# Linear attention and SwiGLU, four layers: attention regrouped through xnᵀφ(k), and a list scheduler for every engine but TensorE

## The chip, the cores and the metric

The kernel runs on one core of one Trainium2 chip. The metric is the device time of one execution in microseconds (us). Five engines work side by side, each through its own instruction queue in order: TensorE (PE; its weight loads are shown as PEld), VectorE (DVE), ScalarE (ACT), GpSimd (POOL) and SyncE (SP), the last of which only issues transfers here. They wait for one another through semaphores.

## What is computed

The input x has 2048 tokens of width 512, in bf16. Two blocks, attention A and feed-forward B, are applied in turn, twice:

```python
x = x + A(layernorm(x));  x = x + B(layernorm(x))
x = x + A(layernorm(x));  x = x + B(layernorm(x))

def A(x):                                 # 32 heads of width 16
    q, k, v = split(x @ wqkv)             # wqkv: 512 x 1536
    phi = lambda t: where(t > 0, t + 1, exp(t)) + 1e-6
    kv = einsum("bhsd,bhse->bhde", phi(k), v)
    z  = einsum("bhsd->bhd", phi(k))
    o  = einsum("bhqd,bhde->bhqe", phi(q), kv) / (phi(q) . z + 1e-6)
    return o @ wo                         # wo: 512 x 512

def B(x):
    return (silu(x @ w_gate) * (x @ w_up)) @ w_down   # 512 x 1792, 1792 x 512
```

The attention is linear: no token-by-token matrix is formed. Per head a 16 x 16 matrix `kv` and a vector `z` are summed over all tokens, and only then can any token's output be formed.

## The kernel before

Tokens are cut into 16 tiles of 128 (`T`), four of which form a group of 512 (`TG` = 4, `G` = 4 groups). Width 512 is cut into `NC` = 4 chunks of 128, the inner width 1792 into `NF` = 14. All weights and X stay in SBUF.

*Norm, for every layer and tile.* DVE takes the statistics (`fe_stats`, L350 and L351). GpSimd forms the reciprocal deviation and the shift for four tiles at once (`fe_rstd`, L361 to L368; for the first four tiles one by one). ACT writes the normalised tile `xn` (`fe_apply`, L378, a ring of four buffers), and a DMA transpose on SP's queue writes it to `xnT` (`fe_T`), the layout that TensorE needs.

*Attention, first pass.* Per tile `p1_proj` (L409) makes k and v, eight matmuls of 512 columns, in banks 0 to 3. phi is ACT's exponential (L388), DVE's min and add (L392), and DVE's max and add (L395). ACT copies v to SBUF (L425). Per group `p1_kvacc_pe` (L443) multiplies phi(k) by v with a column of ones, 16 matmuls of 129 columns, threaded between the projections; DVE adds the four groups' results up. `kv_final` masks the product to the heads' blocks (`KVbd`, `Z8`).

*Attention, second pass.* Per group and chunk `p2_q` (L484) makes q, transposed, in banks 0 and 1; phi follows. `p2_den_pe` (L508, 16 matmuls of 8 columns) makes the denominators, DVE takes the reciprocal (L514, L517), TensorE transposes it (L522), ACT copies it (L528), TensorE spreads it over the heads' rows (L535), and DVE multiplies q by it (L544). `p2_o_pe` (L550) multiplies by `KVbd`, ACT copies the result (L555), and `wo_pe` (L563) multiplies by `Wo`; a fifth matmul with the identity (L566) adds X, and ACT writes X back (L571).

*Feed-forward.* Per group and inner chunk `gu_pe` (L583) makes gate and up, eight matmuls, in one of three pairs of banks. ACT takes tanh(g/2) (L594); DVE forms (tanh + 1) g (L601) and 0.5 times that times up (L604), which is `hT`. After 14 chunks `dn_pe` (L613) makes each tile's 14 down matmuls, and DVE adds X (L620; L624 in the last layer, whose result goes to DRAM).

*What sets the order.* `Tasks.run` walks all tasks in rounds; a task is emitted when all that it depends on were emitted in an earlier round, and each kind has a quota per round. Every engine's queue is then in the order of emission; `Sched` turns reads and writes of named buffers into semaphore waits. TensorE is the engine the rounds are built around: projections, q blocks and gate blocks each wait for their predecessor and for a free ring slot. Weights come in on GpSimd's queue, chunk after chunk behind the first layer's transposes; chunks of one weight share a name, so the next waits for the one before.

## Time and profile before

| | us |
|---|---|
| Times of three runs | 489.0, 490.49, 491.71 |
| Median | 490.49 |
| Profiled execution, span from first to last instruction | 491.9 |
| PE busy | 445.4 |
| DVE busy | 318.2 |
| ACT busy | 207.0 |
| POOL busy | 43.5 |

The profiled execution is another execution than the three timed ones; it has no time of its own beside its span. The span is 1.4 us above the median run. TensorE's matmuls overlap: one of 512 columns is shown with 379 ns, but in a row of them one starts every 216 ns, so a busy TensorE need not be at its peak; elapsed time has to be compared with counts.

### The profile page before, as it was taken

Reading aid. Unit: us, or ns where it says so; the run is one execution under the profiler, and the core shown is the slowest. Engines: PE = TensorE matmul, PEld = TensorE weight load, DVE = VectorE, ACT = ScalarE, POOL = GpSimd, SP = SyncE. Lnnn points to the kernel's source line nnn. Section 1 sums busy time; section 2 is a strip of 40 time slices with the busy share of each in tenths; the row PEclk is TensorE's granted clock in tenths of the full one; section 3 lists DMA queues with packets and bytes.
Section 4 is the critical chain, followed back from the end, with each engine's and each line's share of the span. In section 5 each row is a group of like instructions: output and inputs, shape, how many; then the busy total and the mean of one; then the engine's idle time right before and its main releaser. Section 6 shows DMA issues by size and latency. Waiting matters only on the chain.

```text
span 491.9 us, 6354 instructions
## 1 busy us (share of the span) xinstructions
PE 445.4 (91%) x2196; PEld 203.3 (41%) x2240; DVE 318.2 (65%) x586; ACT 207.0 (42%) x345; POOL 43.5 (9%) x113
## 2 busy tenths in 40 slices
PE   0898758989999999999999975889999999999997
PEld 0343323434344444444444542444434444444443
DVE  4843768728956846846846566872995574573672
ACT  2685434685541511511508643577553131131120
POOL 6431110101200100100101000010120000000000
...
GB/s 296 134 152 157 160 65 0 1 44 17 69 44 0 45 1 1 43 1 0 44 1 45 0 0 1 1 0 45 26 59 65 22 2 23 21 0 23 21 2 43
DMA packets 41135, 20.60 MB, mean 42 GB/s; under 512 B 35408, under 2 KB 39504, under 8 KB 41104
## 3 DMA queue, kind: packets, MB, share of 16 engines
...
q10 hardware_dynamic: 528, 1.57, 0.9%
...
q14 instruction: 13, 0.11, 0.1%
...
## 4 chain that ended last, share of the span: by engine, by line
PE 75%; DVE 12%; DMA 4%; ACT 3%; issue 3%; POOL 2%; POOLq 0%; ACTq 0%; DVEq 0%
PE pb L583 33%; PE pb L613 19%; PE pb L409 10%; DMA sb<-sb 4%; PE pb L563 4%; PE pb L484 3%; DVE sb L395 3%; DVE sb L350 2%; DVE sb L604 2%; DVE sb L601 2%; PE pb L443 1%; DVE sb L544 1%; DVE sb L517 1%; ACT sb L378 1%; PE pb L566 1%
## 5 line engine op out<-in xcount | busy, mean ns | idle before, releaser
L583 PE MATMUL pb<-sb 128*128 128x512 bf16 x879 | 198.0, 379 | 2.3 <-DVE sb L601 1.4
L594 ACT ACTIVATE sb<-pb 128x512 bf16<-128x512 f32 x112 | 66.7, 596 | 168.2 <-PE pb L583 157.9
L583 PEld LDWEIGHTS pb<-sb 128*128 128x128 bf16 x896 | 87.1, 98 | 109.0 <-ACT sb L594 4.2
L613 PE MATMUL pb<-sb 128*128 128x512 bf16 x438 | 100.2, 379 | 0.5
L601 DVE SCALAR_TENSOR_TENSOR sb<-sb,pb 128x512 bf16<-128x512 bf16 x112 | 76.1, 680 | 25.5 <-ACT sb L594 25.5
L409 PE MATMUL pb<-sb 128*128 128x512 bf16 x250 | 65.6, 401 | 17.9 <-DMA sb<-sb 17.2
L604 DVE SCALAR_TENSOR_TENSOR sb<-sb,pb 128x512 bf16<-128x512 bf16 x112 | 76.9, 687 | 3.8
L613 PEld LDWEIGHTS pb<-sb 128*128 128x128 bf16 x448 | 43.8, 98 | 52.8
L388 ACT ACTIVATE sb<-pb 128x512 bf16<-128x512 f32 x64 | 38.2, 596 | 61.2 <-PE pb L484 29.9
L378 ACT ACTIVATE sb<-sb 128x512 bf16<-128x512 bf16 x64 | 51.7, 808 | 14.4 <-POOL sb L368 13.9
L484 PE MATMUL pb<-sb 128*128 128x512 bf16 x123 | 32.8, 387 | 18.5 <-DVE sb L395 17.4
L350 DVE BATCH_NORM_STATS2 sb<-sb 128x6 f32<-128x512 bf16 x64 | 43.4, 678 | 6.9 <-DMA sb<-in_A_x_dram 6.8
L409 PEld LDWEIGHTS pb<-sb 128*128 128x128 bf16 x256 | 25.5, 102 | 52.0 <-issue 21.4
L395 DVE SCALAR_TENSOR_TENSOR sb<-pb,sb 128x512 bf16<-128x512 f32 x64 | 44.3, 692 | 2.2
L624 DVE TENSOR_TENSOR sb<-pb,sb 128x512 bf16<-128x512 f32 x16 | 11.1, 692 | 43.0 <-PE pb L613 43.0
L620 DVE TENSOR_TENSOR sb<-pb,sb 128x512 bf16<-128x512 f32 x16 | 11.1, 692 | 36.4 <-PE pb L613 36.4
L392 DVE TENSOR_SCALAR sb<-sb 128x512 bf16<-128x512 bf16 x64 | 18.1, 282 | 24.6 <-ACT sb L388 24.6
L544 DVE TENSOR_TENSOR sb<-pb,sb 128x512 bf16<-128x512 f32 x32 | 21.9, 684 | 16.2 <-PE pb L535 15.9
L563 PE MATMUL pb<-sb 128*128 128x512 bf16 x124 | 32.1, 379 | 0.1
L361 POOL TENSOR_SCALAR sb<-sb 128x4 f32<-128x4 f32 (+1 forms) x19 | 4.3, 226 | 278.0 <-DVE sb L351 277.7
L484 PEld LDWEIGHTS pb<-sb 128*128 128x128 bf16 x128 | 10.8, 98 | 35.0 <-ACT sb L388 10.8
L443 PE MATMUL pb<-sb 128*128 128x129 bf16 x128 | 23.6, 220 | 1.2 <-DVE sb L395 1.0
...
## 6 DMA issues: line engine op xcount, KB each, us to landing
...
sb<-sb SPq DMA_TRANSPOSE x64, 2.5
...
```

What stands on the lines that cost most here:

```text
L350: op("dve", lambda v: v.bn_stats(stats[:, t, :], Xin[:, t, :]), reads=[f"X{t}"], writes=[f"stats{t}"])
L378: op("act", lambda a: a.activation(out=xn[b][:], in_=Xin[:, t, :], func=ACT.Identity, bias=nmr[:, t:t + 1], scale=rstd[:, t:t + 1]), reads ...
L388: op("act", lambda a: a.activation(out=etmp[e][:], in_=PB[pb][:], func=ACT.Exp), reads=[f"pb{pb}"], writes=[f"etmp{e}"])
L395: op("dve", lambda v: v.scalar_tensor_tensor(out=dst_ap, in0=PB[pb][:], scalar=0.0, in1=etmp[e][:], op0=ALU.max, op1=ALU.add), reads=[f"pb ...
L409: op("pe", lambda pe, pb=pb, col0=col0, c=c: pe.matmul(PB[pb][:], lhsT=xnT[:, c, t * P:(t + 1) * P], rhs=Wqkv[:, c, col0:col0 + 512], star ...
L484: op("pe", lambda pe, c=c: pe.matmul(PB[pb][:], lhsT=Wqkv[:, c, j * P:(j + 1) * P], rhs=xnT[:, c, g * 512:(g + 1) * 512], start=(c == 0), ...
L563: op("pe", lambda pe, c=c: pe.matmul(PB[pb][:], lhsT=oT[ob][:, c, tl * P:(tl + 1) * P], rhs=Wo[:, c, :], start=(c == 0), stop=False), read ...
L583: op("pe", lambda pe, pb=pb, W=W, c=c: pe.matmul(PB[pb][:], lhsT=W[:, c, j * P:(j + 1) * P], rhs=xnT[:, c, g * 512:(g + 1) * 512], start=( ...
L594: op("act", lambda a: a.activation(out=tht[s][:], in_=PB[pbg][:], func=ACT.Tanh, scale=0.5), reads=[f"pb{pbg}"], writes=[f"sg{s}"])
L601: op("dve", lambda v: v.scalar_tensor_tensor(out=gst[s][:], in0=tht[s][:], scalar=1.0, in1=PB[pbg][:], op0=ALU.add, op1=ALU.mult), reads=[ ...
L604: op("dve", lambda v: v.scalar_tensor_tensor(out=hT[hb][:, j, :], in0=gst[s][:], scalar=0.5, in1=PB[pbu][:], op0=ALU.mult, op1=ALU.mult), ...
L613: op("pe", lambda pe, j=j: pe.matmul(PB[pb][:], lhsT=hT[hb][:, j, tl * P:(tl + 1) * P], rhs=Wd[:, j, :], start=(j == 0), stop=(j == NF - 1 ...
```

## The change

Attention is regrouped. Since v = xn Wv, phi(k)ᵀ v is (xnᵀ phi(k))ᵀ Wv; so v is not formed per token. `g_acc` sums G = xnᵀ phi(k) over all 16 tiles in four banks. `kvt` forms Wvᵀ G per chunk and masks it to the heads' blocks, and `m_mm` multiplies that by `Wo`, so that M = KV Wo. z is summed by matmuls with a column of ones (`z_acc`). phi(q) is divided by its denominator before M: the reciprocal is repeated over a head's 16 columns by ACT, transposed by a DMA on SP's queue, and multiplied into phi(q) by DVE (`den`). `wo` then needs four matmuls per tile, and DVE adds X.

The norm's GpSimd part runs per tile. Tiles 0 to 3 of the first layer are normalised by DVE and transposed by TensorE; all others go by DMA transposes as before. Normalised attention tiles are all kept (`xnA`), since `g_acc` reads them; `xnT` becomes six buffers of a group each. Gate and up use four banks (two pairs), k and q two, everything else two. `hT` holds twice the value, the halving is in the residual, and tanh is kept in fp32.

TensorE's order is written out by hand: 14 matmuls on zeros at the start; the last q block and eight `wo` tiles of each attention, and twelve k projections of the third layer, are threaded through the gate blocks. The order on the other engines comes from a list scheduler over modelled durations: at each step the instruction that can start first goes next, ties by a deadline computed back from TensorE's order.

```diff
+    def schedule(self):
...
+        while left:
+            best = None
+            for e in self.ENGINES:
+                if e == "pe":
+                    if pe_at < len(pe_q) and nd[pe_q[pe_at].i] == 0:
+                        o = pe_q[pe_at]
+                        s = max(free[e], rt_of[o.i])
+                        if best is None or s < best[0]:
+                            best = (s, o)
+                    continue
+                cand = None
+                for o in avail[e]:
+                    s = max(free[e], rt_of[o.i])
+                    key = (s, o.dead, o.i)
+                    if cand is None or key < cand[0]:
+                        cand = (key, o)
...
+        r_gu = Ring([0, 1, 2, 3])
+        r_kq = Ring([4, 5])
+        r_tok = Ring([6, 7])
...
+        def ln(L, t, apply="act", pe_t=False):
...
+            if apply == "act":
+                op("pool", lambda p: p.tensor_scalar(out=nmr[:, t:t + 1], in0=mv[:, t, 0:1],
+                                                     scalar1=rstd[:, t:t + 1], scalar2=-1.0,
...
+                op("act", lambda a: a.activation(out=b_ap, in_=X[:, t, :], func=ACT.Identity,
...
+            if pe_t:
+                pb = r_kq.take()
+                tp = PB[pb][:].bitcast(BF16)
+                for c in range(NC):
+                    op("pe", lambda e, c=c: e.transpose(out=tp[:, c * P:(c + 1) * P],
...
+                op("dve", lambda v: v.tensor_copy(out=dst, in_=tp[:, 0:512].rearrange("p (c k) -> p c k", c=NC)),
...
+            else:
+                op("sp", lambda e: e.dma_start(dst, b_ap, transpose=True), r=[bk], w=[f"xt{sl}_{tl}"],
+                   occ=0.1, lat=2.5, dma="t")
...
+        def k_proj(L, t):
...
+                mm(pb, xnT[sl][:, c, tl * P:(tl + 1) * P], Wqkv[:, c, D:2 * D], c == 0, c == NC - 1,
+                   r=[f"xt{sl}_{tl}", "Wk"], w=[f"pb{pb}"])
+            phi(pb, pk[t][:], f"pk{t}", "stt")
+
+        def g_acc(t):
+            for c in range(NC):
+                mm(c, xnA[:, t, c * P:(c + 1) * P], pk[t][:], t == 0, t == T - 1,
+                   r=[f"xa{t}", f"pk{t}"], w=[f"pb{c}"])
...
+        def z_acc(L, tiles):
...
+                    mm(pb, pk[t][:, c * P:(c + 1) * P], ones[:], t == 0 and c == 0, t == T - 1,
...
+        def g_copy():
             for c in range(NC):
+                evac(c, GT[:, c, :], f"GT{c}", "act" if c % 2 == 0 else "dve")
+
+        def kvt():
...
+                    mm(pb, Wqkv[:, k, 2 * D + c * P:2 * D + (c + 1) * P], GT[:, k, c * P:(c + 1) * P],
...
+        def m_mm():
+            for c in range(NC):
+                mm(c, KVT[:, c, :], Wo[:, c, :], True, True, r=["KVT", "Wo"], w=[f"pb{c}"])
+                evac(c, Mo[:, c, :], f"Mo{c}", "act" if c % 2 == 0 else "dve")
...
+        def den(L, g):
...
+            op("dve", lambda v: v.reciprocal(out=rtok[d][:], in_=dsb[d][:]), r=[f"dsb{d}"], w=[f"rtok{d}"],
...
+            for tl in range(TG):
+                q = r_rrep.take()
+                op("act", lambda a, tl=tl, q=q: a.activation(
...
+                op("sp", lambda e, tl=tl, q=q: e.dma_start(RT[R][:, :, tl * P:(tl + 1) * P], rrep[q][:],
+                                                           transpose=True),
...
+            for j in range(NC):
+                b = pq_of[L, g, j]
+                op("dve", lambda v, j=j, b=b: v.tensor_tensor(out=pq[b][:], in0=pq[b][:], in1=RT[R][:, j, :],
...
+        def wo(L, t):
...
+                mm(pb, pq[n][:, tl * P:(tl + 1) * P], Mo[:, c, :], c == 0, c == NC - 1,
...
+        warm = r_tok.take()
+        for i in range(14):
+            mm(warm, zero[:, 0:P], zero, True, True, r=[f"h1_{NF - 1}"], w=[f"pb{warm}"], occ=0.427)
+        for t in range(2):
+            ln(0, t, apply="dve", pe_t=True)
+        late_consts([pr.ops[-1]])
+        for t in range(2, TG):
+            ln(0, t, apply="dve", pe_t=True)
+        for t in range(TG, T):
+            ln(0, t)
+        for w_ in weights[0:2]:
+            w_([])
...
+        for t in range(T):
+            k_proj(0, t)
+            load_next(1)
+            if t >= LAG:
+                g_acc(t - LAG)
+
+        for L in (0, 2):
+            if L == 0:
+                q_proj(L, 0, 0)
+                g_acc(T - 2)
+                q_proj(L, 0, 1)
+                g_acc(T - 1)
+                g_copy()
+                z_acc(L, range(0, T))
+                z_fin(L)
+            q_proj(L, 0, 2)
+            q_proj(L, 0, 3)
+            kvt()
+            q_proj(L, 1, 0)
+            q_proj(L, 1, 1)
+            m_mm()
+            den(L, 0)
+            q_proj(L, 1, 2)
+            q_proj(L, 1, 3)
+            den(L, 1)
+            q_proj(L, 2, 0)
+            q_proj(L, 2, 1)
+            q_proj(L, 2, 2)
+            q_proj(L, 2, 3)
+            for t in range(0, TG):
+                wo(L, t)
+            den(L, 2)
+            for t in range(TG, 2 * TG):
+                wo(L, t)
+            for g in range(G):
+                main = [B(gu, L + 1, g, j) for j in range(NF)] + [B(dn, L + 1, t) for t in range(TG * g, TG * (g + 1))]
+                fill = []
                 if g == 0:
+                    fill += [B(wo, L, t) for t in range(2 * TG, 3 * TG)]
+                    fill += [B(q_proj, L, 3, j) for j in range(NC)] + [B(den, L, 3)]
+                if g == 1:
+                    fill += [B(wo, L, t) for t in range(3 * TG, 4 * TG)]
+                if L == 0 and g >= 1:
+                    fill += [B(k_proj, L + 2, t) for t in range(TG * (g - 1), TG * g)]
+                run(weave(main, fill, 2, NF))
             if L == 0:
+                for t in range(2 * TG, 3 * TG):
+                    g_acc(t - 2 * TG)
+                for t in range(TG, 3 * TG):
+                    g_acc(t)
+                q_proj(2, 0, 0)
+                for t in range(3 * TG, T):
+                    k_proj(2, t)
+                    if t > 3 * TG:
+                        g_acc(t - 1)
+                z_acc(2, range(0, T - 1))
+                q_proj(2, 0, 1)
+                g_acc(T - 1)
+                g_copy()
...
```

Each `wo` tile is followed by the norm of that tile for the feed-forward, and each down tile by the norm for the next attention. The first load is `Wk` (the middle third of `Wqkv`), on ACT's queue; q's and v's thirds come at once on GpSimd's queue, and each later weight chunk waits for the phi of one tile of the first k projection.

1147 lines of the change are left out of this document (465 added, 682 removed).

## The prediction

> **What bounds the kernel now.** I read the totals first, then the stretches, then the chain and the waits in the stretches where TensorE is idle.
>
> The page's totals:
> ```profile
> PE 445.4 (91%) x2196; PEld 203.3 (41%) x2240; DVE 318.2 (65%) x586; ACT 207.0 (42%) x345; POOL 43.5 (9%) x113
> ```
> Busy time by stretch; I cut at the first projection, the last one, the first `Wo` matmul, and the first gate matmul of each layer:
> ```profile
> core 0: us, PE busy (x) PEld busy (x) DVE busy (x) ACT busy (x) POOL busy (x), PEclk, DMA share, GB/s
> 0.00:14.00 14.00, 0.03 (x1) 0.06 (x2) 6.85 (x17) 4.41 (x5) 9.67 (x42) 1.00 0.91 283
> 14.00:53.30 39.30, 35.38 (x173) 16.07 (x177) 21.89 (x51) 26.16 (x44) 11.17 (x21) 0.96 0.69 144
> 53.30:85.70 32.40, 22.37 (x147) 10.19 (x149) 24.76 (x53) 13.06 (x23) 2.22 (x3) 0.95 0.21 69
> 85.70:110.30 24.60, 23.16 (x123) 10.72 (x124) 13.18 (x26) 18.42 (x33) 1.71 (x4) 1.00 0.11 22
> 110.30:256.70 146.40, 144.94 (x659) 65.48 (x672) 102.24 (x175) 50.82 (x81) 10.20 (x24) 1.00 0.12 22
> 256.70:287.30 30.60, 30.43 (x175) 15.09 (x177) 18.58 (x40) 20.59 (x35) 1.70 (x4) 1.00 0.09 18
> 287.30:317.70 30.40, 20.88 (x147) 9.59 (x149) 24.50 (x53) 12.92 (x23) 0.00 (x0) 1.00 0.01 1
> 317.70:342.30 24.60, 23.03 (x122) 10.69 (x124) 13.14 (x26) 18.42 (x33) 1.70 (x4) 1.00 0.13 23
> 342.30:488.90 146.60, 145.19 (x660) 65.37 (x671) 92.34 (x147) 42.23 (x69) 5.11 (x12) 1.00 0.10 25
> 488.90:491.90 3.00, 0.00 (x0) 0.00 (x0) 0.69 (x1) 0.00 (x0) 0.00 (x0) 0.85 0.13 44
> ```
> Prices of TensorE's work, from the chain of waits (first two rows) and the timeline:
> ```profile
> 144.20 3.02 PE pb L613 x14
> 29.60 0.06 PE pb L443
> ...
> 64.00 0.55 PE L508 MATMUL pb<-sb 128*128 128x8 bf16 x16
> 64.41 1.02 PE L484 MATMUL pb<-sb 128*128 128x512 bf16 x4
> ...
> 67.75 0.60 PE L522 MATMUL pb<-sb 128*32 128x128 f32 x4
> 68.18 1.03 PE L484 MATMUL pb<-sb 128*128 128x512 bf16 x4
> ```
> A 512-column matmul takes 3.02/14 = 0.2157 us, one of 129 columns 0.06, one of 8 columns 0.41/16 = 0.026, a small transpose 0.43/4 = 0.108. The loops issue 1952 + 128 + 128 + 32 of these: 421.0 + 7.7 + 3.3 + 3.5 = 435.5 us of work in a span of 491.9. So 56.4 us are lost. By stretch, elapsed minus work: 14.0 before the first matmul; 8.8 in the first k/v pass; 12.0 and 10.0 in the two q stretches; 2.6 twice in the `Wo` stretches; 1.5 and 1.6 in the MLPs; 0.1 in the second k/v pass; 3.0 at the end. TensorE's own work is the bound of the MLPs; the losses lie in the attention layers.
>
> Chain of waits at the start, and one row of the waits:
> ```profile
> 7.33 0.82 ACT sb L378
> 8.17 5.66 DMA sb<-sb
> 13.97 4.93 PE pb L409 x12
> 18.91 5.83 DMA sb<-sb
> ...
> 36.29 7.44 DMA sb<-sb
> 43.86 5.50 PE pb L409 x17
> ```
> ```profile
> PE pb L484 <- DVE sb L395: 17.4, 15, 2.3
> ```
> The first pass loses time to DMA transposes that land late beside the loads, and to a half clock: the first 12 matmuls took 4.93/12 = 0.41 us each. The q stretches wait for DVE's phi: 15 waits, 1.16 us each.
>
> **The change, part by part.** *TensorE's work.* Per attention layer the v projection and `KV` (64 + 64 short) become `g_acc` (64), `z_acc` (64 of one column), `kvt` (16 of 128) and `m_mm` (4); the reciprocal's transposes, its spreading (16), `o` (16) and X through the identity (16) go. q, the k projection, `den` and 64 `Wo` matmuls stay. Wide ones fall from 304 to 260, so 1864 in all, with the MLPs' 1344 unchanged: 402.1 us. `kvt` costs 32 x 0.06 = 1.9 and `den` 3.3. No row has a one-column matmul; it lies between nothing and the 0.06 row, nearest to the 8-column row: 128 x 0.026 = 3.3. Total 410.6, that is 24.9 us less (bounds 20.5 to 28.2).
>
> *Start.* Tiles 0 to 3 are transposed on TensorE and the first load is `Wk`, a third of `Wqkv`. But TensorE's queue is in order, and the first projection stands behind all four tiles.
> ```profile
> 5.79 0.24 POOL L361 TENSOR_SCALAR sb<-sb 128x1 f32<-128x1 f32 x1
> 6.12 0.58 POOL L364 TENSOR_TENSOR sb<-sb 128x1 f32<-128x1 f32 x1
> ...
> 7.76 0.69 DVE L350 BATCH_NORM_STATS2 sb<-sb 128x6 f32<-128x512 bf16 x1 [3.80 <-DMA sb<-in_A_x_dram]
> ...
> 8.58 0.66 DVE L350 BATCH_NORM_STATS2 sb<-sb 128x6 f32<-128x512 bf16 x1
> ...
> 9.38 0.66 DVE L350 BATCH_NORM_STATS2 sb<-sb 128x6 f32<-128x512 bf16 x1
> ```
> Four tiles and `Wk` are 1.0 MB, about 3.5 us at the 283 GB/s of the first stretch; with a share for the other queues tile 3 is there at about 6.7. Statistics (0.8), GpSimd (two steps, 5.79 to 6.70, about 0.9), normalising, transposing and copying add 2.8: first projection at 9.5 (bounds 8 and 13, the latter if tile 3 comes as late as now). Fourteen zero matmuls at about 0.41 us run from 1.5 to some 6 us and pay the slow clock early, which saves 12 x (0.41 - 0.216) = 2.3 if the clock holds across the gap. The 17 matmuls at 43.86 follow a gap of 2.3 us and took 0.32 each, so it may not. The Trainium skill, "TensorE: Matmul & The Clock Gate", Part 1 and Part 4, says the clock halves after an idle window of about 3.4 us and that transposes do not count as activity; by that the 2.3 us would be paid again at 9.5.
>
> *First pass.* Projections and `g_acc` alternate, 1.73 us per tile. Twelve tiles still go by DMA transposes beside 13 weight loads, each now released by a tile's phi and up to four in flight on the GpSimd queue, where the LN arithmetic of later tiles stands behind them. Loss between 1 (transposes run ahead, no ring of four `xn` buffers holds them) and the present 9: I take 4.
>
> *The stretch from g to the first gate matmul.* The MLP gets q block 3 and eight `wo` tiles as filling; here stay 12 q projections, `kvt`, `m_mm`, three `den` and eight `wo`. DVE rows:
> ```profile
> L395 DVE SCALAR_TENSOR_TENSOR sb<-pb,sb 128x512 bf16<-128x512 f32 x64 | 44.3, 692 | 2.2
> L544 DVE TENSOR_TENSOR sb<-pb,sb 128x512 bf16<-128x512 f32 x32 | 21.9, 684 | 16.2 <-PE pb L535 15.9
> L392 DVE TENSOR_SCALAR sb<-sb 128x512 bf16<-128x512 bf16 x64 | 18.1, 282 | 24.6 <-ACT sb L388 24.6
> L517 DVE RECIPROCAL sb<-sb 128x128 f32<-128x128 f32 x8 | 7.6, 954 | 0.3
> ```
> Back to back they overlap a little (timeline, DVE):
> ```profile
> 164.25 0.68 DVE L601 SCALAR_TENSOR_TENSOR sb<-sb,pb 128x512 bf16<-128x512 bf16 x1
> 164.97 0.69 DVE L604 SCALAR_TENSOR_TENSOR sb<-sb,pb 128x512 bf16<-128x512 bf16 x1
> 165.57 0.68 DVE L601 SCALAR_TENSOR_TENSOR sb<-sb,pb 128x512 bf16<-128x512 bf16 x1
> ```
> so an independent one occupies 0.60 to 0.61, a gate/up pair 1.32, and a tile's statistics 0.80 (8.58 to 9.38). A phi is 0.28 + 0.61 = 0.89. The new product of q with the reciprocal has both inputs in SBUF as bf16: no row; between 0.28 (L392) and 0.68 (L544, from PSUM); I take 0.35, nearest to L392. "VectorE: DVE Perf Modes" of the Trainium skill, in its perf-mode tier table, gives such a product two results per cycle, an estimated 0.33 us; the sum would not move by 1 us.
>
> DVE: 12 phi 10.7, evictions of G and M and the mask 3.0, `z_fin` 0.2, three `den` with four products each 3 x (0.28 + 0.95 + 1.4) = 7.9, eight residuals with statistics 8 x 1.41 = 11.3; sum 33.1. TensorE in the same stretch: 12 q and 2 g 12.1, z 1.7, `kvt` and M 1.9, `den` 1.2, `wo` 6.9; 23.8. DVE is the bound: loss 9.3, taken as 10 (3 if statistics slip into the MLP, 15 if DVE fills 85% only; the q stretches now fill 76 and 81%). In layer 2 the two first q, two g and z lie earlier: 31.1 against 18.7, loss 12. The residual moves from ACT to DVE, v's copies and `o`'s go; ACT has room.
>
> *Reciprocals.* `den`, reciprocal, four ACT copies, four DMA transposes, four products. Of transposes:
> ```profile
> L99 SPq DMA_TRANSPOSE sb<-sb x64: 1188/1191/2302, 8.2 to 375.7; - x64
> sb<-sb SPq DMA_TRANSPOSE x64, 2.5
> ```
> SP's queue takes 1.19 us for each, in order with LN's. The chain is 0.28 + 0.95 + 0.6 + 4 x 1.19 + 1.3 + 1.4 = 9.3 us; from `den(0)` to `wo(0)` DVE has 9.2 us to do (two reciprocals with their additions 2.5, six phi 5.3, the products 1.4). It is hidden, barely, and only because DVE is the bound.
>
> *MLPs.* Four instead of six banks for gate and up. With filling, group 0 has on DVE 14 x 1.32 + 4 x 1.41 + 4 x 0.89 + 2.6 = 30.3 us against 24.2 + 6.9 + 0.4 = 31.5 on TensorE, and statistics left over from `wo` may spill in; group 1 of layer 1 is as tight. I take 5 and 4 us (bounds 1.5, as now, and 20). *Layer 1 to 2:* 12 `g_acc` (10.4 us) cover the last tiles' norm and transposes (residual 0.7, statistics 0.8, GpSimd 1, ACT 0.8 as in the L378 row, DMA 2.5); 2 lost. *End:* unchanged, 3.0.
>
> Sum: 410.6 + 9.5 + 4 + 10 + 5 + 2 + 12 + 4 + 3 = 460.1 as a span. The profiled span of 491.9 is 1.4 us above the median run, 490.49; so 458.7, say 459.
>
> **The rivals.** *A, DVE's surplus is absorbed.* Statistics and products are done in the down projections, where DVE has 12.1 us with 4 x 1.41 of work. For it: the MLP stretch shows DVE busy 102 of 146 us. Against it: `wo` needs the products at once. Losses 9 + 2 + 4 + 2 + 1 + 5 + 2 + 3 = 28: span 438.6, time 437.
>
> *B, the smaller ring holds the MLP.* This row gives ACT's part:
> ```profile
> L594 ACT ACTIVATE sb<-pb 128x512 bf16<-128x512 f32 x112 | 66.7, 596 | 168.2 <-PE pb L583 157.9 <-DVE sb L350 5.7 <-DVE sb L601 4.7
> ```
> An up bank is free 0.86 + 0.16 + 0.60 + 0.71 + 0.69 + 0.1 = 3.1 us after its block began; two blocks on, it is wanted at 4.3 (with three pairs at 6.0). A residual with statistics (1.4) in between exceeds the slack of 1.2 by 0.2: over 112 blocks 22 us, of which 6 are counted: 475. For it: PE's waits on DVE exist already with three pairs. Against it: half the blocks have no filling. "Perfetto Trace Analysis" of the Trainium skill (Identifying Performance Opportunities) reads a repeating gap on the saturated engine as too few buffers; no run here shows it in the MLP.
>
> *C, slower: head of line on DVE.* DVE's order is fixed from modelled times. An instruction that stands at its head with a late operand holds every gate product behind it. Place: the MLPs' groups with filling. Price: 1.16 us, the mean wait of the L484 row. It decides from 33/1.16 = 28 such events beyond those counted, one in four gate blocks; at 40 the time is 505. Against it: TensorE's order is fixed too, and lateness moves all queues alike.
>
> *D, no change:* the same at about 28 events; 490. That the change does not remove the work it says is excluded by the counted loops.
>
> **How the numbers follow.** Forecast 0.42 (its own range 448 to 470), A 0.27, B 0.18, C 0.09, D 0.04. The range 434 to 484 leaves out a little of A and B, and C and D. No change means within 0.5% (488 to 493), about what can be told apart here: faster 0.87, same 0.04, slower 0.09.
>
> **What would show it.** Right: about 1864 wide matmuls; first projection near 9.5 us; in the stretch from the last projection to the first gate matmul DVE over 85% busy and PE waiting for DVE; MLPs near 171 and 160 us. Wrong: PE waits on DMA transposes in front of `wo`, or a gap in nearly every gate block (B), or DVE waiting for ACT or DMA while PE waits for DVE (C), or those stretches near 25 us (A).

## The result, and the profile after

The changed kernel takes 475.98 us (median of 4 runs, 473.24 to 478.77); the kernel before, run beside it, 491.1 (489.0 to 492.85). The ratio is 0.9687, 95% interval 0.9621 to 0.9752: 3.1% faster. The forecast was 459 us, a gain of 31.5; measured are 15.1. The sign is right and the size is missed by half.

Totals of the page, and busy time by stretch, of the changed kernel. The cuts are the first projection, the first q block, the first gate of layer 1, the first `g_acc` of layer 2, the third q block of layer 2, the first gate of layer 3 and the last matmul; the columns are those of the table of before.
```profile
PE 435.2 (91%) x2182; PEld 194.2 (41%) x2182; DVE 327.8 (69%) x613; ACT 171.6 (36%) x277; POOL 77.2 (16%) x214
```
```profile
0.00:15.30 15.30, 6.68 (x31) 3.17 (x32) 7.37 (x21) 0.86 (x1) 6.87 (x23) 0.86 0.75 240
15.30:48.44 33.14, 28.62 (x123) 11.37 (x122) 20.96 (x51) 18.42 (x29) 18.04 (x46) 0.96 0.82 168
48.44:89.35 40.91, 30.42 (x222) 13.43 (x221) 32.01 (x70) 18.29 (x33) 7.36 (x19) 0.83 0.34 90
89.35:257.50 168.15, 167.96 (x784) 75.89 (x785) 127.44 (x223) 64.97 (x102) 26.88 (x77) 0.99 0.14 27
257.50:279.66 22.16, 21.09 (x154) 9.91 (x153) 6.73 (x14) 5.32 (x9) 1.32 (x4) 1.00 0.09 17
279.66:315.95 36.29, 24.25 (x146) 9.90 (x144) 29.28 (x66) 17.31 (x31) 5.84 (x18) 0.86 0.22 44
315.95:473.60 157.65, 156.22 (x736) 70.56 (x736) 103.36 (x169) 46.40 (x76) 10.93 (x31) 1.00 0.13 30
473.60:477.00 3.40, 0.00 (x0) 0.00 (x0) 0.69 (x1) 0.00 (x0) 0.00 (x0) 1.00 0.11 39
```
Elapsed minus TensorE's work (0.2157 us for each wide matmul, the forecast's prices for the others) is the loss of a stretch:

| stretch | elapsed | work | loss | forecast |
|---|---|---|---|---|
| start | 15.3 | 0 | 15.3 | 9.5 |
| first pass | 33.1 | 25.9 | 7.2 | 4 |
| layer 0, q to first gate | 40.9 | 23.8 | 17.1 | 10 |
| MLP of layer 1 | 168.2 | 166.1 | 2.0 | 5 |
| layer 1 to 2 | 22.2 | 20.6 | 1.6 | 2 |
| layer 2, q to first gate | 36.3 | 18.7 | 17.6 | 12 |
| MLP of layer 3 | 157.7 | 155.7 | 1.9 | 4 |
| end | 3.4 | 0 | 3.4 | 3 |

The whole miss lies in four rows: 5.8 + 3.2 + 7.1 + 5.6 = 21.7 us, less 5.5 that the two MLPs and the stretch from layer 1 to 2 do better. In the q stretches TensorE's granted clock is 0.83 and 0.86, where the kernel before had 0.95 and 1.00, and DVE is busy 78 and 81% of the time.

What TensorE waits for in layer 0's stretch (waits view; total, times, longest), and what DVE waits for there:
```profile
PE pb L343 <- DVE pq L459: 4.4, 6, 2.6
PE pb L343 <- DMA xnT<-xnB: 2.3, 1, 2.3
PE pb L343 <- DVE pq L562: 2.3, 1, 2.3
PE pb L343 <- ACT etmp L454: 0.8, 1, 0.8
PE pb L343 <- DVE X L573: 0.8, 1, 0.8
```
```profile
DVE etmp L456 <- ACT etmp L454: 7.4, 8, 1.8
```
Ten waits make 10.6 of the 17.1 us. Most of the rest is half clock behind the long ones: in three rows, 8, 4 and 16 wide matmuls take 3.57, 1.86 and 6.26 us, together some 5.6 us more than at 0.2157 each. DVE itself is kept waiting by ACT's exponentials. The timeline shows the longest wait as a chain through four queues (start, duration, in brackets the idle time before and its releaser):
```profile
62.55 2.19 ACT L553 ACTIVATE rrep<-rtok 128x512 bf16<-128x512 f32 x4 [0.83 <-DVE rtok L548]
...
64.64 0.57 ACT L454 ACTIVATE etmp<-pb 128x512 bf16<-128x512 f32 x1
65.25 0.29 DVE L456 TENSOR_SCALAR etmp<-etmp 128x512 bf16<-128x512 bf16 x1 [1.79 <-ACT etmp L454]
65.64 0.69 DVE L459 SCALAR_TENSOR_TENSOR pq<-pb,etmp 128x512 bf16<-128x512 f32 x1
66.39 0.27 PE L343 MATMUL pb<-Zm,pq 128*128 128x8 bf16 x4 [2.62 <-DVE pq L459]
66.52 3.57 PE L343 MATMUL pb<-xnT,Wqkv 128*128 128x512 bf16 x8
...
70.29 1.86 PE L343 MATMUL pb<-xnT,Wqkv 128*128 128x512 bf16 x4 [0.20 <-DVE pq L459]
```
ACT's four copies of the reciprocals stand in front of the exponential of q(1,3). DVE waits 1.79 us for that exponential, TensorE 2.62 us for DVE, and the next eight wide matmuls take 3.57 us in place of 1.73, at half clock. Another chain of this kind ends at the first gate:
```profile
78.79 1.28 DVE L408 BATCH_NORM_STATS2 stats<-X 128x6 f32<-128x512 bf16 x2
...
80.03 7.96 SPq L445 DMA_TRANSPOSE xnT<-xnB  x4
80.24 0.87 POOL L410 TENSOR_SCALAR vpe<-mv 128x1 f32<-128x1 f32 x3 [1.19 <-DVE mv L409]
80.28 1.09 DVE L562 TENSOR_TENSOR pq<-pq,RT 128x512 bf16<-128x512 bf16 x3
80.76 6.26 PE L343 MATMUL pb<-Mo,pq 128*128 128x512 bf16 x16 [2.26 <-DVE pq L562]
81.07 1.76 POOL L413 TENSOR_TENSOR rstd<-vpe,negh 128x1 f32<-128x1 f32 x3
...
82.93 0.74 POOL L422 TENSOR_SCALAR nmr<-mv,rstd 128x1 f32<-128x1 f32 x3
83.29 2.22 ACT L426 ACTIVATE xnB<-X,nmr,rstd 128x512 bf16<-128x512 bf16 x3 [3.33 <-POOL nmr L422]
...
89.35 1.71 PE L343 MATMUL pb<-xnT,Wg 128*128 128x512 bf16 x4 [2.33 <-DMA xnT<-xnB]
```
The products of group 1 start at 80.28, behind the residuals and statistics of earlier tiles, so `wo(4)` waits 2.26 us and its 16 matmuls run at half clock (6.26 us for 3.45 of work). The norm of tiles 1 to 3 needs 3.4 us on GpSimd, step by step for three tiles, then ACT, then SP, and the gate comes 11 us after `wo(3)`.

### The profile page after: what moved, and what is told of

Same layout as the page of the kernel before. It is cut to its first block, busy times and chain, and to the rows that moved or that the text cites. A ratio compares the mean times of both kernels' runs of the same rounds, so it can differ in the third digit from the quotient of the medians.

```text
span 477.0 us, 6447 instructions
## 1 busy us (share of the span) xinstructions
PE 435.2 (91%) x2182; PEld 194.2 (41%) x2182; DVE 327.8 (69%) x613; ACT 171.6 (36%) x277; POOL 77.2 (16%) x214
## 4 chain that ended last, share of the span: by engine, by line
PE 73%; DVE 9%; DMA 7%; SPq 5%; POOL 2%; issue 2%; ACT 2%; DVEq 0%; ACTq 0%; POOLq 0%
PE pb L343 72%; DMA xnT<-xnA 3%; SPq L557 3%; DMA RT<-rrep 2%; SPq L445 2%; DVE stats L408 2%; DVE pq L459 2%; DVE X L573 1%; DMA X<-in_A_x_dram 1%; POOL rstd L413 1%; DVE pq L562 1%; ACT etmp L454 1%; DVE etmp L456 1%; POOL vpe L410 1%; DVE Mo L500 1%
## 5 line engine op out<-in xcount | busy, mean ns | idle before, releaser
L343 PE MATMUL pb<-xnT,Wg 128*128 128x512 bf16 x448 | 115.8, 381 | 5.5 <-DMA xnT<-xnB 5.3
L343 PE MATMUL pb<-xnT,Wu 128*128 128x512 bf16 x448 | 115.9, 381 | 1.4 <-DVE hT L596 1.4
L591 ACT ACTIVATE tht<-pb 128x512 f32<-128x512 f32 x112 | 66.5, 595 | 124.5 <-PE pb L343 112.9
L343 PE MATMUL pb<-Wd,hT 128*128 128x512 bf16 x448 | 98.0, 379 | 0.0
L593 DVE SCALAR_TENSOR_TENSOR tht<-tht,pb 128x512 f32<-128x512 f32 x112 | 76.5, 683 | 26.3 <-ACT tht L591 25.7
L596 DVE TENSOR_TENSOR hT<-tht,pb 128x512 bf16<-128x512 f32 x112 | 76.8, 686 | 9.8 <-DVE mv L409 0.4
L343 PEld LDWEIGHTS pb<-xnT,Wg 128*128 128x128 bf16 x448 | 43.8, 98 | 59.6 <-issue 7.4
L343 PEld LDWEIGHTS pb<-xnT,Wu 128*128 128x128 bf16 x448 | 44.0, 98 | 55.2 <-DVE hT L596 2.1
L343 PEld LDWEIGHTS pb<-Wd,hT 128*128 128x128 bf16 x448 | 43.7, 98 | 52.4
L454 ACT ACTIVATE etmp<-pb 128x512 bf16<-128x512 f32 x64 | 37.9, 594 | 64.4 <-PE pb L343 57.5
L408 DVE BATCH_NORM_STATS2 stats<-X 128x6 f32<-128x512 bf16 x64 | 42.8, 682 | 7.4 <-DMA X<-in_A_x_dram 6.6
L343 PE MATMUL pb<-Mo,pq 128*128 128x512 bf16 x128 | 36.1, 419 | 6.0 <-DVE pq L562 4.5
L426 ACT ACTIVATE xnB<-X,nmr,rstd 128x512 bf16<-128x512 bf16 x32 | 25.3, 809 | 36.8 <-POOL nmr L422 30.6
L343 PE MATMUL pb<-pk,xnA 128*128 128x512 bf16 x128 | 31.1, 379 | 0.0
## 6 DMA issues: line engine op xcount, KB each, us to landing
Wu<-in_B_w_up_dram POOLq DMA_DIRECT2D x4, 448.0 KB, 10.7
```

The lines of the kernel that those rows point to most:

```text
L343: return op("pe", lambda e: e.matmul(o_ap, lhsT=lhsT, rhs=rhs, start=start, stop=stop, skip_group_check=skip), r=r, w=w, occ=occ, lat=occ ...
L408: op("dve", lambda v: v.bn_stats(stats[:, t, :], X[:, t, :]), r=[xk], w=[f"st{t}"], occ=0.6)
L426: op("act", lambda a: a.activation(out=b_ap, in_=X[:, t, :], func=ACT.Identity, bias=nmr[:, t:t + 1], scale=rstd[:, t:t + 1]), r=[xk, f"nm ...
L454: op("act", lambda a: a.activation(out=etmp[e][:], in_=PB[pb][:], func=ACT.Exp), r=[f"pb{pb}"], w=[f"e{e}"], occ=0.485, lat=0.6)
L591: op("act", lambda e: e.activation(out=tht[a][:], in_=PB[pg][:], func=ACT.Tanh, scale=0.5), r=[f"pb{pg}"], w=[f"th{a}"], occ=0.485, lat=0.6)
L593: op("dve", lambda v: v.scalar_tensor_tensor(out=tht[a][:], in0=tht[a][:], scalar=1.0, in1=PB[pg][:], op0=ALU.add, op1=ALU.mult), r=[f"pb{ ...
```

## The experiments

Two theories stood at first: L, that the reciprocals' chain and the half clock behind its waits make the surplus loss, and D, that DVE's load does, as the forecast had it. Each kernel was timed beside the kernel before, in 4 runs (6 for e1). Where stretches are compared they are differences of the starts of the same matmuls in one profiled execution each:

| kernel | median us | ratio, 95% interval | start | first pass | layer 0: q to gate | layer 2: second q block to gate |
|---|---|---|---|---|---|---|
| changed kernel | 475.98 | 0.9687 (0.9621-0.9752) | 15.3 | 33.2 | 40.9 | 38.1 |
| a1 | 475.94 | 0.9671 (0.9629-0.9713) | 14.7 | 31.2 | 40.9 | 38.1 |
| a2 | 471.92 | 0.9589 (0.9556-0.9622) | 15.3 | 35.4 | 38.0 | 34.2 |
| a3 | 483.87 | 0.9839 (0.9813-0.9865) | 15.2 | 35.6 | 42.4 | 40.1 |
| a4 | 474.59 | 0.9662 (0.9618-0.9705) | 15.2 | 31.0 | 42.6 | 37.8 |
| b1 | 475.95 | 0.9666 (0.9624-0.9707) | 15.3 | 30.9 | 40.6* | 37.6* |
| b2 | 470.08 | 0.9559 (0.9496-0.9622) | 15.2 | 33.6 | 35.2* | 33.6* |
| b3 | 480.29 | 0.9770 (0.9697-0.9843) | 12.4 | 38.6 | 41.0 | 37.9 |
| b4 | 473.51 | 0.9629 (0.9589-0.9669) | 15.2 | 29.2 | 43.1 | 37.6 |
| c1 | 470.24 | 0.9577 (0.9531-0.9622) | 15.0 | 33.0 | 41.1* | 30.6* |
| c2 | 468.30 | 0.9527 (0.9478-0.9576) | 15.1 | 29.4 | 40.6* | 30.6* |
| c3 | 466.06 | 0.9479 (0.9437-0.9522) | 12.5 | 29.1 | 39.4* | 30.6* |
| c4 | 471.48 | 0.9591 (0.9550-0.9632) | 15.3 | 29.2 | 40.3* | 33.1* |
| d1 | 500.66 | 1.0214 (1.0151-1.0277) | 18.3 | 44.8 | 44.5 | 42.0 |
| d2 | 477.26 | 0.9725 (0.9650-0.9800) | 15.3 | 30.9 | 40.7 | 37.5 |
| d3 | 474.44 | 0.9649 (0.9594-0.9704) | 14.7 | 37.2 | 38.7* | 32.1* |
| d4 | 476.40 | 0.9684 (0.9622-0.9745) | 13.1 | 34.8 | 41.9* | 34.0* |
| e1 | 459.75 | 0.9353 (0.9312-0.9394) | 12.4 | 29.2 | 36.1* | 30.7* |
| e2 | 463.19 | 0.9434 (0.9390-0.9479) | 12.4 | 29.6 | 40.1* | 30.1* |

\* less the work that was moved into the stretch from the MLP (3.45 us; in d4 another 3.86).

The first pass is not steady: where nothing bearing on it was changed (changed kernel, a2, a3, b1, b2) it took 30.9 to 35.6 us. That is why the stretches are looked at and not the medians alone.

### First round: one suspect each

**a1**, the first loads in program order:
```diff
-                    key = (s, o.dead, o.i)
+                    key = (s, o.i if o.dma == "d" else o.dead, o.i)
```


> The list scheduler's choice among ready loads goes by the order in which they are written instead of by deadline; so tile 0 is loaded first instead of fourth (in the changed kernel the deadlines put tiles 3, 2, 1, 0 in this order on SP's queue, and DVE's first statistics, those of tile 0, wait until 7.8 us). If the order of the loads holds the start: the statistics of tiles 0 to 2 are done by the time the fourth load lands at about 7.8, and the first projection comes at about 11.8 instead of 15.3 us; the time falls by 3 to 4 us (ratio to the changed kernel about 0.993). If the last of the four loads or the bandwidth holds it, whatever the order: first projection at 15, time unchanged within 1 us.

The order of the loads alone is worth 0.6 us of start. Tile 0's statistics came at 3.07 us (7.82 in the changed kernel), but DVE's timeline shows what took their place:
```profile
8.55 0.38 DVE L430 TENSOR_SCALAR xnA<-X,mv,rstd 128x512 bf16<-128x512 bf16 x1
10.68 0.69 DVE L408 BATCH_NORM_STATS2 stats<-X 128x6 f32<-128x512 bf16 x1 [1.75 <-DMA X<-in_A_x_dram]
11.29 0.40 DVE L430 TENSOR_SCALAR xnA<-X,mv,rstd 128x512 bf16<-128x512 bf16 x1
```
The statistics of tile 4, whose load lands at 10.7, stand at the head of DVE's queue in front of tile 1's normalisation.

**a2**, no division: the copies, their transposes and the four products of `den` are left out, so q is not divided.
```diff
-            R = r_RT.take()
-            for tl in range(TG):
...
```


> Leaves out the division: after the reciprocal there are no ACT copies, no transposes by DMA and no products, so q goes to M undivided. Theory L (latency: the two stretches from q to the first gate matmul are long because TensorE waits for the reciprocal chain and for what stands behind its ACT copies, and runs at half clock after each wait): those stretches fall from 40.9 and 36.3 us to about 31 and 27, time minus 18 us or more. Theory D (DVE's load is the bound, as forecast): only the products are saved on DVE, 3 x 1.42 us in each stretch and as much spread over the MLPs, time minus 9 us or less.

The stretches fall by 2.9 and 4.0 us. TensorE's waits of 2.62 and 2.26 us go, and a longer one at the gate appears (the waits view of a2):
```profile
PE pb L343 <- DMA xnT<-xnB: 10.7, 2, 5.4
```
It was 5.3 us for both layers in the changed kernel. Of the 9.8 us of waits that go in the two layers, 5.4 come back in front of the gate. The time falls by 4.1 us, far from L's 18 and within what D allowed; that DVE's load is the reason is not shown by this, since the longer wait at the gate accounts for it as well.

**a3**, matmuls that nobody reads, added in front of the three waits of each attention layer:
```diff
+            keep_clock(10)
             den(L, 1)
...
+            keep_clock(9)
             for t in range(TG, 2 * TG):
                 wo(L, t)
+            keep_clock(11)
```


> Adds 30 matmuls of 512 columns per attention layer, whose result nobody reads, at the three places where TensorE waits over 2 us: 10 before the second group's denominators, 9 before the wo tiles of the second group, 11 before the first gate matmul. 60 matmuls are 12.9 us of work, placed where TensorE stands idle anyway. Theory L: the waits themselves stay, but the half clock behind them goes (granted clock 0.83 and 0.86 in the two stretches, above 0.95 then); time minus 6 to 10 us. Theory D: DVE sets the pace, a faster TensorE only waits longer; time within 1 us, or longer by what the added matmuls overrun.

The half clock went, as L expected: in layer 0's stretch the granted clock is 1.00. But the 30 matmuls cost 6.5 us a layer, the stretches grow by 1.5 and 2.0 us, and the gate still waits behind them:
```profile
86.19 2.54 PE L343 MATMUL pb<-Wo 128*128 128x512 bf16 x11
93.17 1.21 PE L343 MATMUL pb<-xnT,Wg 128*128 128x512 bf16 x4 [4.44 <-DMA xnT<-xnB]
```
Filling a wait with useless work is no gain; the chains themselves end no sooner. Less the work added, the stretches are 36.0 and 33.6 us (40.9 and 38.1 in the changed kernel); the difference is the half clock, together with waits that the added work filled.

**a4**, one more DVE instruction for each q block, which nobody waits for:
```diff
+            op("dve", lambda v: v.tensor_scalar(out=hT[1][:, NF - 1, :], in0=Wo[:, 0, :], ...
```


> Adds to each of the 32 q blocks one DVE instruction that nobody waits for (min and add over 128 x 512 bf16, 0.28 us, 0.20 where it overlaps); 12 of them fall into the stretch from q to the first gate matmul of layer 0, 10 into that of layer 2. Theory D: each stretch grows by what is added, 2.4 to 3.4 us, time plus 5 to 6.5 us. Theory L: DVE is busy 32.0 of 40.9 and 29.3 of 36.3 us there and takes them in its idle time; time plus 2 us at most.

No change, but this tells less than it was meant to. The 32 instructions depend on nothing in the stretch, and the scheduler put them where DVE was free: the view of these instructions has none of them between the first q block and the first gate of layer 0 (count, duration, first and last start).
```profile
L535 DVE TENSOR_SCALAR hT<-Wo x32: 260/293/347, 27.9 to 262.1; 128x512 bf16<-128x512 bf16 x32
```
So DVE's load isn't refuted by a4. It is by b2 below.

### Second round: order, start, loads

Theory N from here on: the serial chains through queues of fixed order set the stretch, not one engine's load.

**b1**, the last four q blocks in front of the first gate, not among the MLP's fillings:
```diff
+            for j in range(NC):
+                q_proj(L, 3, j)
...
-                    fill += [B(q_proj, L, 3, j) for j in range(NC)] + [B(den, L, 3)]
+                    fill += [B(den, L, 3)]
```


> One move: in both attention layers the four blocks q(3,0) to q(3,3) (16 matmuls, 3.45 us) are issued right behind wo(7) and no longer among the fillings of the MLP's first group. No work is added. Theory N (the end of the stretch is set by the serial chain wo(3), residual, statistics, GpSimd, ScalarE, SyncE's transpose, some 11 us long, with only den(2) and wo(4) to wo(7) of TensorE work behind it): the waits of 2.33 and 3.02 us in front of the first gate and the half clock behind them go, the MLPs get 3.45 us shorter each: 6 to 8 us faster than the changed kernel, about 469. Rival R (the other engines' work up to the first gate sets it, in whatever order TensorE stands): four more phi blocks stand ahead of the chain on ScalarE and VectorE (0.49 + 0.85 us each), the gate comes later by what was moved: within 1.5 us of the changed kernel, about 476, with a wait of 2 us or more still in front of the first gate.

Rival R holds: net of the moved work the stretches are 40.6 and 37.6 against 40.9 and 38.1. The norm's chain ends later by what stands ahead of it.

**b2**, another order in the middle of the stretch:
```diff
             kvt()
             q_proj(L, 1, 0)
+            den(L, 0)
             q_proj(L, 1, 1)
             m_mm()
-            den(L, 0)
             q_proj(L, 1, 2)
             q_proj(L, 1, 3)
-            den(L, 1)
             q_proj(L, 2, 0)
             q_proj(L, 2, 1)
+            den(L, 1)
             q_proj(L, 2, 2)
             q_proj(L, 2, 3)
             for t in range(0, TG):
                 wo(L, t)
             den(L, 2)
+            for j in range(NC):
+                q_proj(L, 3, j)
             for t in range(TG, 2 * TG):
                 wo(L, t)
...
-                    fill += [B(q_proj, L, 3, j) for j in range(NC)] + [B(den, L, 3)]
+                    fill += [B(den, L, 3)]
```


> The same work, only TensorE's written order of the stretch is changed: q(0,2), q(0,3), kvt, q(1,0), den(0), q(1,1), M, q(1,2), q(1,3), q(2,0), q(2,1), den(1), q(2,2), q(2,3), wo(0) to wo(3), den(2), q(3,0) to q(3,3), wo(4) to wo(7). Each link that TensorE waited for now has work behind it: two q blocks between q(1,3) and den(1); some 7.3 us from den(0) to wo(0), 9 us from den(1) to wo(4), 6.9 us and no den from wo(3) to the first gate. Theory N: the waits of 2.62, 2.26 and 2.33 us (2.62, 2.26, 3.02 in layer 2), each with some 2.8 us of half clock behind it, go but for 1 to 3 us in front of wo(0) or the gate: 15 to 22 us faster than the changed kernel, 454 to 461. Rival R: the waits move, their sum stays: 473 to 478.

Here the stretches shrink by 5.7 and 4.5 us net, with DVE's work unchanged; so its load is not what set them. The whole kernel gains 5.9. That is a third of what N expected, and the waits are nearly those that R expected: in layer 0 they still sum to 9.3 us (10.6 before). But they are cut into shorter ones, and the granted clock is 1.00 throughout. So of the 5.7 us, 1.3 are waits, and most of the rest is the half clock behind them. The waits of layer 0's stretch in b2:
```profile
PE pb L343 <- DVE pq L459: 6.7, 7, 2.4
PE pb L343 <- DMA xnT<-xnB: 1.8, 1, 1.8
PE pb L343 <- DVE X L573: 0.5, 2, 0.4
PE pb L343 <- ACT Mo L497: 0.3, 1, 0.3
```
**b3**, a1 with the statistics of tile 4 and later held back until tile 3 is copied:
```diff
+        last = [pr.ops[-1]]
         for t in range(TG, T):
-            ln(0, t)
+            ln(0, t, after=last)
```


> As a1_first_loads (tile 0 is loaded first), and the statistics of tile 4 and later wait until the last of the first four tiles is transposed and copied, so that VectorE's fixed order can't put them ahead. Theory N: the first projection stood behind the load of tile 4 on VectorE; without that it comes at 11 to 12.5 us (15.3 in the changed kernel, 14.7 in a1_first_loads), 2.5 to 4 us faster than the changed kernel, 472 to 473.5. Rival: tiles 4 to 15 are then normalised too late and the first pass waits for their transposes: the gain of the start is given back there, 475 to 478.

The first projection comes at 12.4 us, 2.9 sooner; the first pass gives back 5.4, as the rival said (waits of b3 in the first pass):
```profile
PE pb L343 <- DMA xnT<-xnA: 4.0, 1, 4.0
PE pb L343 <- DVE mv L409: 2.6, 1, 2.6
```
**b4**, later weight loads:
```diff
-            load_next(1)
+            load_next(1 if t >= 8 else 0)
...
             if L == 0:
+                load_next(5)
```


> The weight loads (Wo, Wg, Wu, Wd) are released one a tile from the ninth tile on and the last five behind the pass, in place of one a tile from the first tile on. Theory T (transposes that share the DMA engines with weight loads land late): the waits of 1.32 and 0.79 us for transposes in the first pass go, and some of VectorE's waits there: 2 to 3.5 us faster than the changed kernel, 472.5 to 474. Rival: the loads now share the DMA engines with the transposes of the stretch, whose waits grow by what the pass gained: 475 to 478; or the transposes' time is their own and the waits stay.

TensorE no longer waits for transposes in the first pass, which takes 29.2 us against the 30.9 to 35.6 of the same code elsewhere. Layer 0's stretch is 2.2 us longer, as the rival had it, but a4, which put nothing there, shows nearly as much (42.6), so that is not settled. The issue rows up to the end of the first pass, with the median from issue to landing, of the changed kernel and then of b4:
```profile
xnT<-xnA SPq DMA_TRANSPOSE x12, 3.6
```
```profile
xnT<-xnA SPq DMA_TRANSPOSE x12, 2.4
```
### Third round: banks, and the gains together

**c1**, b2 with six PSUM banks for the q blocks in place of two:
```diff
+        r_q6 = Ring([4, 5, 0, 1, 2, 3])
...
-            pb = r_kq.take()
+            pb = (r_kq if g == 0 and j < 2 else r_q6).take()
```


> b2_order with six PSUM banks in place of two for the q blocks of the stretch (the four of G and M are free there), no work added. In b2_order TensorE still waited 6.7 us in layer 0's stretch for a phi that had to free one of the two banks (longest 2.41 and 1.52 us). Theory K (turnaround of two banks: matmuls, exponential, two VectorE steps, some 2.8 us a block against 0.86 us of matmuls): these waits go and only what den, wo and the gate need is waited for; the stretches get 3 to 5 us shorter each, 6 to 9 us faster than b2_order, 461 to 464. Rival V (VectorE does the phi blocks, products and residuals no faster, 28.4 us busy in b2_order's 33.4 us): TensorE runs ahead and then waits the same time in front of wo(0), wo(4) or the gate: within 2 us of b2_order, 468 to 472.

No gain in the time, and two opposite effects in the stretches: layer 2 falls by 3.0 us, layer 0 rises by 5.9. M's four results have fixed banks, of which the ring had just given two to q(1,0) and q(1,1):
```profile
60.45 0.81 PE L344 MATMUL pb<-Wo,KVT 128*128 128x512 bf16 x2 [1.42 <-DVE pq L460]
62.27 6.59 PE L344 MATMUL pb<-xnT,Wqkv 128*128 128x512 bf16 x16 [1.01 <-ACT Mo L498]
```
Two short waits in a row, and 16 matmuls at half clock, 3.1 us too long: together 5.5 of the 5.9 us.

**c2**, c1 with b4's loads; **c3**, c2 with b3's start, tile 4 being held back only until tile 3 is normalised:

> c1_order_banks with the weight loads of b4_wload. If the first pass's gain (4 us there, of which 2.5 showed in the time) is independent of the stretch: 2.5 to 4 us faster than c1_order_banks. If the five late loads slow the stretch's transposes: no gain.

> c2_banks_wload with the start of b3_start, except that the statistics of tile 4 wait for the normalisation of tile 3 only and not for its copy. In b3_start the first projection came at 12.4 us (15.3 before), and 2.6 us were lost again in front of tile 4's projection and 4.0 us in front of a transpose beside weight loads; the second can't come here, since the loads are later. Theory N: 1 to 3 us faster than c2_banks_wload. Rival: the first pass waits for the transposes of tiles 4 to 7, whatever the loads do: 0 to 2 us slower.

Both gain about 2 us. With the loads out of the way the sooner start is kept: 12.5 and then 29.1 for the pass.

**c4**, c2 with two feed-forward tiles transposed on TensorE just ahead of the first gate. Only three buffers hold normalised tiles, so by then tiles 5 and 6 lie in those of tiles 2 and 3 and are transposed in their place:
```diff
-            ln(L + 1, t)
+            ln(L + 1, t, pe_t="late" if t in (2, 3) else False)
```


> c2_banks_wload with the normalised feed-forward tiles 2 and 3 transposed on TensorE right in front of the first gate (8 transposes, 0.5 us, and two VectorE copies of 0.42 us) and not by SyncE. Theory N (the LN chain's last links, 2.4 to 3.6 us from SyncE's issue to landing, set the first gate): the wait in front of it falls by 1 to 2 us, net of the transposes 1 to 3 us faster for both layers. Rival: VectorE's in-order copies come as late as the DMA's landing: within 1 us.

3.2 us slower than c2. As it waits for tiles that are ready later, it does not decide about N; that stays untried.

### Fourth round: the list scheduler's own choices

**d1**, GpSimd tile by tile:
```diff
-                    key = (s, o.dead, o.i)
+                    key = (max(s, free[e] + 0.35), 0.0, o.i) if e == "pool" else (s, o.dead, o.i)
```


> The changed kernel with one line of the list scheduler changed: on GpSimd, operations that can start within 0.35 us of each other are taken in program order (all three steps of a tile, then the next tile) and not by the earliest start, which put the first step of three tiles, then the second of three, then the third of three (0.87, 1.76 and 0.74 us in front of the first gate). Theory N (GpSimd's order is a link of the chain to the first gate): xnB of tile 1 is ready 2 us sooner, SyncE's three issues of 1.28 us start sooner, the wait of 2.3 to 3.0 us in front of the first gate and the half clock behind it go: 4 to 8 us faster than the changed kernel, 468 to 472. Rival: the last tile's three steps end when they ended before, and the gate needs the last tile: within 2 us.

24.7 us slower than the changed kernel, which neither side expected. The line moves all of GpSimd's queue, the weight loads' issues too: none of those that the pass releases goes out before 31.8 us, when four follow one another, and the later transposes of the first pass share the DMA engines with them. The chain of waits of d1, in the first pass:
```profile
35.86 0.81 ACT xnA L426
36.70 0.03 issue
36.73 16.91 DMA xnT<-xnA
```
One transpose took 16.9 us to land, TensorE waited 7.1 and 4.4 us in the pass, and both stretches lengthened by over 3 us. It confirms b4 from the other side; whether GpSimd's order by itself matters in the stretch, d1 cannot say.

**d2**, the true price of a transpose on SP's queue in the scheduler:
```diff
-                   occ=0.1, lat=2.5, dma="t")
+                   occ=1.22, lat=2.5, dma="t")
```


> The changed kernel, with the list scheduler told that a transposing DMA holds SyncE's queue for 1.22 us, as the trace shows, and not 0.1 us. Theory N' (a wrong price puts transposes that nobody waits for yet, those of the next group's reciprocals, ahead of the feed-forward tiles): 2 to 5 us faster, 471 to 474. Rival: the order on SyncE's queue follows from when the sources are ready, whatever the price: within 2 us.

Nothing: stretches 40.7 and 37.5. **d3** is c3 with d1's and d2's edits, and **d4** is d3 with den(3) and `wo(8)` to `wo(11)` in front of the gate:

> c3_start (TensorE's order, six banks, late weight loads, tile 0 first) with the GpSimd order of d1_depth and the SyncE price of d2_sp_price. In c3_start TensorE still waited 4.2 and 3.4 us in front of the first gates. Theory N: these waits shrink by 2 us or more each, with the half clock behind them: 4 to 8 us faster than c3_start, 458 to 462. Rival (VectorE's statistics of tiles 1 to 3 come too late in any case): within 2 us.

> d3_all with den(3) and wo(8) to wo(11) (3.9 us of TensorE work) in front of the first gate and not in the MLP's first group. Theory cover (what is left is latency that more TensorE work hides): the first gate no longer waits, 2 to 4 us faster than d3_all. Rival: wo(8) waits for its own reciprocals instead, den(2) being only 6.9 us ahead of it and the chain 9.3 us long: no faster than d3_all.

In d3 the stretches change by -0.7 and +1.5 us, and the first pass loses 8 us to d1's late loads. In d4 they are 3.2 and 1.9 us longer than in d3, and the gate of layer 0 still waits 2.67 us: more cover, like b1's, only moves the wait.

**e1**, c3 with M in the ring of six banks:
```diff
             for c in range(NC):
-                mm(c, KVT[:, c, :], Wo[:, c, :], True, True, r=["KVT", "Wo"], w=[f"pb{c}"])
-                evac(c, Mo[:, c, :], f"Mo{c}", "act" if c % 2 == 0 else "dve")
+                pb = r_q6.take()
+                mm(pb, KVT[:, c, :], Wo[:, c, :], True, True, r=["KVT", "Wo"], w=[f"pb{pb}"])
+                evac(pb, Mo[:, c, :], f"Mo{c}", "act" if c % 2 == 0 else "dve")
```


> c3_start with M's four results taken from the same ring of six banks as the q blocks, so that they fall into banks freed long before and not into the two that q(1,0) and q(1,1) hold. Theory K (turnaround of PSUM banks, and the collision in layer 0): the waits of 1.43 and 1.01 us at M and the half clock over the 16 matmuls behind them (5.31 us in place of 3.45) go, layer 0's stretch falls from 42.9 to 37 to 40 us, layer 2's stays at 34.1 or falls by up to 1: 3 to 6 us faster than c3_start, 460 to 463. Rival V (VectorE or ScalarE sets the stretch): the wait comes back at den(1) or wo(0): within 1.5 us of c3_start, 464.5 to 467.5.

459.75 us, 0.9353 (0.9312 to 0.9394): faster than both kernels. The waits at M are gone, and layer 0's stretch falls by 3.3 us. That is nearly all of the 3.6 us between the two profiled executions (464.76 and 461.2); the medians lie 6.3 apart, because c3's profiled execution was its fastest and e1's its second slowest, and what the others did no trace shows. Its stretches (same cuts as above):
```profile
...
12.43:41.61 29.18, 27.86 (x121) 11.60 (x121) 21.98 (x55) 18.19 (x28) 17.16 (x45) 0.95 0.58 137
41.61:81.20 39.59, 30.18 (x238) 14.48 (x236) 32.55 (x72) 20.44 (x36) 8.93 (x19) 0.94 0.51 137
...
269.62:301.91 32.29, 24.15 (x161) 10.84 (x159) 29.67 (x68) 19.06 (x34) 4.39 (x12) 1.00 0.25 50
```
Start 12.4, first pass 29.2 - 25.9 = 3.3, layer 0 39.6 - 27.3 = 12.3, layer 2 32.3 - 22.2 = 10.1 (q(3,0) to q(3,3) are counted in the work). In layer 2 the clock is full and DVE is busy 92% of the time.

**e2**, e1 with two of a group's four copies on GpSimd:
```diff
+                    op("pool", lambda g, r_ap=r_ap, t_ap=t_ap: g.tensor_copy(out=r_ap, in_=t_ap), ...
```


> e1_m_ring with two of the four copies of the reciprocals of a group made by GpSimd and not by ScalarE. What GpSimd takes for such a copy no trace shows; its nearest rows are 0.20 us for a memset of 128x128 and 0.30 to 0.35 us for a masked select of 128x128, which by size make 0.8 to 1.4 us for 128x512. Theory S (exponentials wait on ScalarE behind copies): den(1)'s and the bank waits shrink by 1 us each: 1 to 3 us faster than e1_m_ring. Rival: GpSimd's copies take over 2 us or slow VectorE, and the products wait for them: 0 to 4 us slower than e1_m_ring.

Layer 2 gains 0.6 us, layer 0 loses 3.9. The copy costs GpSimd 653 ns, hardly more than ACT's 626, but in layer 0 it stands behind weight loads whose issue waits for an earlier load, and wo waits up to 7.4 us for the product:
```profile
49.33 0.76 POOL L370 DMA_DIRECT2D Wd<-in_B_w_down_dram  x1 [5.16 <-DMA Wu<-in_B_w_up_dram]
...
58.04 0.75 POOL L370 DMA_DIRECT2D Wd<-in_B_w_down_dram  x1 [3.45 <-DMA Wd<-in_B_w_down_dram]
58.78 1.24 POOL L563 CAST rrep<-rtok 128x512 bf16<-128x512 f32 x2
```

## Why the prediction was right or wrong

**TensorE's work, 410.6 us: right.** The two MLP stretches, counted with the same prices, lose 2.0 and 1.9 us. The one-column matmul, which had no row, takes 1.60/64 = 0.025 us (0.026 was taken), the product of q four in 1.42 us, 0.355 each (0.35).

**MLPs, 171 and 160 us: 168.2 and 157.7.** Two pairs of banks suffice; rivals B and C, as they were placed in the MLPs, are refuted there. That B's time, 475, is the measured one is a coincidence: its 22 us lay in the MLPs, which lose 2.0 and 1.9.

**Layer 1 to 2 and the end: right** within 0.4 us.

**Start, 9.5 us: 15.3.** The step that failed is the arrival of the tiles: they were taken to land in order, tile 3 at 6.7, and DVE to take them one after another. The scheduler's deadlines loaded them backwards, tile 0 last. But a1 shows that this alone is 0.6 us; statistics of a later tile, at the head of DVE's queue, cost another 2.3. With both mended (b3, c3) it is 12.4 or 12.5. The other 2.9 us are in b3's timeline:
```profile
7.56 0.69 DVE L408 BATCH_NORM_STATS2 stats<-X 128x6 f32<-128x512 bf16 x1 [0.98 <-DMA X<-in_A_x_dram]
...
12.41 3.57 PE L343 MATMUL pb<-Wqkv,xnT 128*128 128x512 bf16 x8
```
Tile 3 is there 0.9 us later than forecast, and from its statistics to the first projection 4.9 us go by in place of 2.8, since tiles 0 to 3 are still normalised, transposed and copied one after another behind them. The slow clock was paid again: in the changed kernel the first eight matmuls of the projections took 3.17 us, 0.40 each; ahead of them TensorE idled for 5.3 us and then did only 16 transposes in 4.1 us. The Trainium skill, "TensorE: Matmul & The Clock Gate", Parts 1 and 4, has the clock halved after an idle window of about 3.4 us, and transposes not counting as a busy TensorE in the same way; the trace agrees.

**First pass, 4 us: 7.2.** The mechanism was named, late transposes beside weight loads; the size was taken too small (5.0 to 9.7 between profiles of the same code). With later loads it is 3.3 (b4: 29.2 - 25.9), with loads and transposes crowded together 18.9 (d1: 44.8 - 25.9).

**The q stretches, 10 and 12 us: 17.1 and 17.6.** DVE's work was summed rightly, 33.1 and 31.1 against 32.0 and 29.3 measured. The step that failed is the next: "DVE is the bound". It was to be busy over 85% of the time there and is 78 and 81%. A bound engine must be fed, and this one waits 7.4 us for ACT in layer 0. b2 cut 4.5 to 5.7 us from the stretches without taking an instruction from DVE. What the timeline shows instead are chains through queues of fixed order, each with its head of line (work that is late or not yet wanted stands ahead of work that is): ACT's copies ahead of an exponential, residuals and statistics ahead of the products, GpSimd's three steps and SP's 1.2 us issues ahead of the gate. Three of these end in a wait over 2 us, and the clock halves. For this half clock the forecast had no term in these stretches. In layer 0 the waits alone, 10.6 us, come near the 10 that were forecast, which is luck, since they end these chains and not a full DVE; the half clock puts some 5.6 us on top. b2, which keeps the clock and 9.3 us of waits, is 5.7 us shorter.

The forecast had the chains as rival C, but put them into the MLPs, where there is slack, and not into the stretch where every link is wanted at once. That the reciprocals are "hidden, barely" held for their transposes in both groups: the last of group 1 was issued at 73.9 us and landed some 2.4 us later. It did not hold for group 1's products, which DVE took up at 80.28 only, so that `wo(4)` waits 2.26 us; that is DVE's order and not the chain's length. Leaving out copies, transposes and products gains only 4 us (a2), since the gate's chain is right behind.

How far the reasoning went shows in e1: with the same matmuls, in another order, other banks and with later loads, its start and first pass lose 15.7 us and its two stretches 22.4, where the forecast had 13.5 and 22; there DVE comes to 92% in layer 2. The forecast priced what the work allows and took the written order to reach it. That e1's time of 459.75 us falls on the forecast's 459 is luck in part, since the start and the pass take more than forecast and the MLPs less.

Rival A fell with the stretches at 36 to 41 us in place of 25.

What stays open: which link of the chains is worth how much, since b2 and e1 moved several at once; why e1's executions differ by 5.6 us among themselves; the waits of 3.2 us that are left in front of e1's two first gates; and what GpSimd's order is worth by itself.
